# Layer 1's weights decoded on a fixed plan of steps: the scale product half a piece behind its maximum, the staging reloaded when the sign is taken

## The chip, the cores and the metric

One Trainium2 chip, one core. The metric is device time in microseconds (us): the median of several executions of the whole kernel. TensorE (PE; PEld is its weight load) multiplies, VectorE (DVE) and ScalarE (ACT) work elementwise, GpSimd (POOL) too but more slowly, and SyncE (SP) issues the transfers; each works off its own queue in order.

## What is computed

Attention with queries pooled by two, then two dense layers in a row. All inputs come as float64 and are kept to nearly float32 accuracy.

```python
# q, k, v: (4, 8, 1152, 64)
q_pool = q.reshape(B, H, S // 2, 2, D).mean(axis=3)
attn = softmax(q_pool @ k.T / sqrt(D))
x = (attn @ v).transpose(0, 2, 1, 3).reshape(2304, 512)
h = x @ w_in;   x = (h * cos(h)) @ w_out       # layer 1: 512 -> 2048 -> 512
h = x @ w_in2;  out = (h * sigmoid(h)) @ w_out2  # layer 2
```

## The kernel before, in words

Attention runs over 16 pairs of heads (four batches, four pairs each), each pair in nine tiles of 128 pooled queries, 144 tiles in all. A tile's scores are products of float16 halves (L545, L553), VectorE takes them out of PSUM with their minimum (L564), ACT makes the exponential (L572) and its high half (L578), POOL the low half (L583), SP transposes both (L585, `hl` to `hlT`), and four tiles later (`LAG`) TensorE multiplies them with v (L596, L600); after three tiles `group_end` divides and stores (L608 to L619).

Before a pair can start, `pair_prep` must have taken the maxima of its q, k and v (L120 to L482, tile `pm`), sent them through a product with a constant matrix (`scale_steps`, L104, tile `bm`) to get one scale for all partitions (L107 to L115), split q, k and v into halves (L460 to L509) and transposed them (L511, L521). This is spread over the tiles of the pair before.

The weights of layer 1 are 16 pieces of 1024 KB in float64: pieces 0 to 7 are of w_in, 8 to 15 of w_out. Each is loaded into one of three staging buffers (`wst`, L186) and decoded by `weight_steps`: ACT takes the absolute value of the upper word (L216, into `wt`) and low bits (L221); VectorE takes the maximum (L217), shifts the low bits in (L227) and the sign (L230); `mw` is the maximum as a number (L92), and its product `bm` gives the scale (L104 to L115); ACT writes the high half (L250) and the scaled value (L251), POOL the low half (L252). A `wt` buffer is held from L216 to L252; there are two of them.

Background work is a list of generators. `advance()` takes one step of each; it is called four times a tile, so a step is a quarter of a tile. The order in which instructions go into each engine's queue is made by a scheduler from their places in the program as priorities and from when they are ready. Products that share the PSUM tag "h" (two buffers) are the scale products of weights and pairs, and later layer 1's first products.

Before, a weight piece takes four steps: `decode(i + 1)` (three) and then `write(i)` (one), so the generator is through after 64 steps, 16 tiles. Layer 1 itself begins when the first block of attention's output is complete, in the 37th tile; `block_done` then calls `finish(wg)`.

Of the kernel before, what the change touches and what calls it, by code (L numbers as in the profile page):

```python
# [26 lines left out]
PSH = 15.0  # L27
NB_N, NB_SC, NB_H, NB_T, NB_S = 2, 4, 4, 4, 5
X_LAG = 40
W1_SUB, W1_BUFS, W1_AHEAD, WT_BUFS = 1, 3, 1, 2  # L30
W2_BUFS, W2_PACE = 3, 6
W2_TABLE = (("i", 0, 11, (0, 2, 5, 7, 10)), ("o", 88, 6, (0, 1, 3, 4, 6, 8, 9)))
PREP_POOL, GH_ACT, GH_TAIL = 0, 0, 0
# [3 lines left out]
R_AT = 1  # L37
NB_HK, NB_TT, NB_G, SIN_N = 2, 2, 2, 2
RATE = (0, 2, 2, 2)
LG, W_PACE, HI_N, HI_A = 12, 1, 2, 2  # L40
LAG = 4
GT = 3
TAIL_G = 4
# [4 lines left out]
def attention_moe_moe_kernel(ctx, tc, q, k, v, w_in1, w_out1, w_in2, w_out2, out):  # L48
# [3 lines left out]
    nc = tc.nc  # L52
# [30 lines left out]
    def scale_steps(m, pool, res, top, wide=False, apart=False, clean=False):  # L83

        n = m.shape[1]
        if wide:
            w = small.tile([128, 1], F32, name="mw", tag="mw")  # L90
            wi, mi = w.bitcast(I32), m.bitcast(I32)
            nc.vector.tensor_scalar(  # L92
                out=wi, in0=mi, scalar1=3, scalar2=EXP_MASK if clean else 0x3F800000, op0=ALU.logical_shift_left,
                op1=ALU.bitwise_and
            )
            if not clean:
                nc.vector.scalar_tensor_tensor(
                    out=wi, in0=mi, scalar=1 << 30, in1=wi, op0=ALU.bitwise_and, op1=ALU.bitwise_or
                )
            m = w  # L100
            if apart:
                yield
        bc = pool.tile([128, 2, GW], F32, tag="h", name="bm")[:, 0, 0:4]
        nc.tensor.matmul(bc[:, 0:n], mean, m, start=True, stop=True)  # L104
        yield
        s, u = res
        nc.vector.tensor_scalar(  # L107
            out=u, in0=bc[:, 0:n], scalar1=TINY, scalar2=2.0**(9 - top), op0=ALU.max, op1=ALU.mult
        )

        nc.vector.tensor_scalar(
            out=s.bitcast(I32), in0=u.bitcast(I32), scalar1=EXP_MASK, scalar2=EXP_MASK,
            op0=ALU.bitwise_and, op1=ALU.bitwise_xor,
        )
        nc.vector.tensor_scalar(  # L115
            out=u.bitcast(I32), in0=u.bitcast(I32), scalar1=EXP_MASK, scalar2=None, op0=ALU.bitwise_and
        )

    def absmax(out_, in_, axis=AX.X):
        nc.vector.tensor_reduce(out=out_, in_=in_, axis=axis, op=ALU.max, apply_absolute_value=True)  # L120
# [9 lines left out]
    def early(g, n):  # L130
        while True:
            with ahead(n):
                r = next(g, END)
            if r is END:
                return
            yield r
# [24 lines left out]
        w.ug = const.tile([128, 1], F32, name="ug" + tag)  # L161
        return w

    def weight_steps(w, srcs, stage, pspool, eng, nsub, bufs, ahead, wt_bufs=WT_BUFS):

        npc = w.npc  # L170
        wide = srcs[0].dtype != F32
        z = 2 if wide else 1
        srcs = [x.bitcast(I32) if wide else x for x in srcs]
        todo = [("i", p, h) for p in range(npc) for h in range(nsub)]
        todo += [("o", p, h) for p in range(npc) for h in range(nsub)]
        staged = []

        def shape(kind):
            return (NC // nsub, DFF // npc) if kind == "i" else (NF // nsub, DM // npc)

        def more():
            if todo:
                kind, p, h = todo.pop(0)
                c, n = shape(kind)
                st = stage.tile([128, c, n, z], I32 if wide else F32, tag="wst", name="wst", bufs=bufs)
                eng.dma_start(  # L186
                    out=st.rearrange("p c f z -> p c (f z)"),
                    in_=srcs[kind == "o"][c * 128 * h:c * 128 * (h + 1), p * n * z:(p + 1) * n * z].rearrange(
                        "(c p) f -> p c f", p=128
                    ),  # L190
                )
                staged.append(st)

        for _ in range(bufs):
            more()
        yield
        pieces = [(kind, p) for kind in "io" for p in range(npc)]
        decoded = []

        def decode(kind, p):  # L200
            c, n = shape(kind)
            s, u = (w.si, w.ui) if kind == "i" else (w.so, w.uo)
            s, u = s[:, p:p + 1], u[:, p:p + 1]
            m = small.tile([128, nsub], F32, name="wm", tag="wm", bufs=3)
            sts = [staged.pop(0) for _ in range(nsub)]
            ts = []
            for h, st in enumerate(sts):
                if not wide:
                    ts.append(st[:, :, :, 0])
                    absmax(m[:, h:h + 1], ts[-1], AX.XY)  # L210
                    yield
                    continue
                t = stage.tile([128, c, n], F32, tag="wt", name="wt", bufs=wt_bufs)
                ti = t.bitcast(I32)
                hf, low = st.bitcast(F32)[:, :, :, 1], st[:, :, :, 0]
                nc.scalar.activation(out=t, in_=hf, func=AF.Abs, scale=2.0**16)  # L216
                nc.vector.tensor_scalar(  # L217
                    out=t, in0=t, scalar1=W_MIN * 2.0**16, scalar2=None, op0=ALU.max, op1=ALU.max,
                    accum_out=m[:, h:h + 1]
                )  # L220
                nc.scalar.activation(  # L221
                    out=low, in_=st.rearrange("p c f z -> p c (f z)").bitcast(U16).rearrange(
                        "p c (f z) -> p c f z", z=4
                    )[:, :, :, 1], func=AF.Identity, scale=2.0**-13, bias=floor3
                )
                yield
                nc.vector.scalar_tensor_tensor(  # L227
                    out=ti, in0=ti, scalar=3, in1=low, op0=ALU.logical_shift_left, op1=ALU.bitwise_or
                )
                nc.vector.scalar_tensor_tensor(  # L230
                    out=ti, in0=st[:, :, :, 1], scalar=-(1 << 31), in1=ti, op0=ALU.bitwise_and, op1=ALU.bitwise_or
                )
                ts.append(t)
                yield
            m1 = m
            if nsub > 1:
                m1 = small.tile([128, 1], F32, name="wm1", tag="wm1", bufs=3)
                nc.vector.tensor_reduce(out=m1, in_=m, axis=AX.X, op=ALU.max)
            for _ in early(scale_steps(m1, pspool(), (s, u), 14, wide, clean=wide), P_CH):
                pass  # L240
            decoded.append(ts)
            yield

        def write(kind, p):
            c, n = shape(kind)
            hw, lw = (w.ih, w.il) if kind == "i" else (w.oh, w.ol)
            s = (w.si if kind == "i" else w.so)[:, p:p + 1]
            for h, t in enumerate(decoded.pop(0)):
                hi, lo = (x[:, c * h:c * (h + 1), p * n:(p + 1) * n] for x in (hw, lw))
                nc.scalar.activation(out=hi, in_=t, func=AF.Copy, scale=s)  # L250
                nc.scalar.activation(out=t, in_=t, func=AF.Copy, scale=s)  # L251
                nc.gpsimd.tensor_tensor(out=lo, in0=t, in1=hi, op=ALU.subtract)  # L252
                more()
                yield
            if (kind, p) == ("i", npc - 1):
                w.half = True

                nc.vector.tensor_reduce(out=w.kg, in_=w.si, axis=AX.X, op=ALU.min)
                nc.vector.tensor_reduce(out=w.ug, in_=w.ui, axis=AX.X, op=ALU.max)
                nc.vector.tensor_scalar(out=w.kg, in0=w.kg, scalar1=2.0**-15, scalar2=None, op0=ALU.mult)  # L260
                nc.vector.tensor_scalar(out=w.ug, in0=w.ug, scalar1=2.0**12, scalar2=None, op0=ALU.mult)

        for i in range(ahead):
            yield from decode(*pieces[i])
        for i, x in enumerate(pieces):
            if i + ahead < len(pieces):
                yield from decode(*pieces[i + ahead])
            yield from write(*x)

        r = npc // NC  # L270
        for e in range(r):
            pp = slice(e * (128 // r), (e + 1) * (128 // r))
            nc.vector.tensor_copy(w.uoT[pp, :], w.uo.rearrange("p (c e) -> p c e", e=r)[pp, :, e])
# [603 lines left out]
    if True:  # L877
# [76 lines left out]
        for n in range(2):  # L954
            P[n] = pair_new(at, *pairs[n])
            run_all(pair_loads(P[n]))
            if n == 0:
                wg = weight_steps(W1, (w_in1, w_out1), wst, lambda: ps_h, nc.sync, W1_SUB, W1_BUFS, W1_AHEAD)
                next(wg)
                run_all(pair_prep(at, P[0]))  # L960

# [2 lines left out]
                for _ in range(n):  # L964
                    yield

        wg = early(slowly(wg, W_PACE), P_W)
        bg.append(wg)

        def prep_then_load(n):  # L970
# [295 lines left out]
```

## Time and profile before

| | |
|---|---|
| median of 3 runs | 1396.19 us (1389.43 to 1397.52) |
| the profiled execution | 1396.53 us, its span 1394.7 us |
| PE busy | 1143.4 us (82%) |
| DVE busy | 1041.5 us (75%) |
| ACT busy | 871.6 us (62%) |
| POOL busy | 610.9 us (44%) |

The busy shares are means over stages that differ: in the first 280 us there is attention of the first batch and the weights of layer 1, then attention and layer 1 together, and from about 840 us on the dense layers.

### The profile page before, as it was taken

Reading aid. Unit: us, or ns where it says so; the run is one execution under the profiler, and the core shown is the slowest. Engines: PE = TensorE matmul, PEld = TensorE weight load, DVE = VectorE, ACT = ScalarE, POOL = GpSimd, SP = SyncE. Lnnn points to the kernel's source line nnn. Section 1 sums busy time; section 2 is a strip of 40 time slices with the busy share of each in tenths; the row PEclk is TensorE's granted clock in tenths of the full one; section 3 lists DMA queues with packets and bytes.
Section 4 is the critical chain, followed back from the end, with each engine's and each line's share of the span. In section 5 each row is a group of like instructions: output and inputs, shape, how many; then the busy total and the mean of one; then the engine's idle time right before and its main releaser. Section 6 shows DMA issues by size and latency. Waiting matters only on the chain. (4 is left out here: it accounts for less than half of the span.)

```text
span 1394.7 us, 26446 instructions
## 1 busy us (share of the span) xinstructions
PE 1143.4 (82%) x10668; PEld 915.2 (66%) x10668; DVE 1041.5 (75%) x1927; ACT 871.6 (62%) x1061; POOL 610.9 (44%) x352
## 2 busy tenths in 40 slices
PE   2464355588898778898898989999898999999998
PEld 1243133366676456666666767888787888888887
DVE  6976897769788689877999897796756764444483
ACT  5867686668686678768678876453636643343352
POOL 2457365527556655665665645433567400000000
PEclk9566568889999978999999999999999999999999
DMA  9899759986989999989699986332336000000001
GB/s 287 176 224 211 204 102 196 201 163 118 187 151 185 200 204 176 201 171 175 135 198 210 200 159 137 91 92 76 76 76 152 31 24 15 25 17 16 17 31 31
DMA packets 509593, 186.26 MB, mean 134 GB/s; under 512 B 465952, under 2 KB 484384, under 8 KB 509472
## 3 DMA queue, kind: packets, MB, share of 16 engines
q1 hardware_dynamic: 509472, 184.59, 64.2%
q8 instruction: 83, 1.36, 0.4%
q14 instruction: 38, 0.31, 0.1%
HBM read 66.58 MB, written 9.44 MB: 55 GB/s over the span
## 5 line engine op out<-in xcount | busy, mean ns | idle before, releaser
L583 POOL TENSOR_TENSOR hl<-sc,hl 128x1152 f16<-128x1152 f32 x144 | 363.6, 2534 | 212.5 <-ACT hl L578 119.1
L545 PE MATMUL sp<-kT,qT 128*128 128x512 f16 (+1 forms) x768 | 196.6, 375 | 98.1 <-DVE sc L564 83.0
L564 DVE TENSOR_SCALAR_CACHE_REDUCE sc<-sp,psu 128x512 f32<-128x512 f32 (+1 forms) x288 | 229.1, 808 | 39.5 <-PE sp L545 34.3
L596 PE MATMUL pv<-vt,hlT 128*128 128x130 f16 (+1 forms) x1440 | 196.7, 238 | 73.5 <-DMA hlT<-hl 66.4
L681 PEld LDWEIGHTS <-ih 128*128 128x128 f16 x2304 | 226.0, 99 | 40.7 <-issue 10.6
L572 ACT ACTIVATE sc<-sc,nb 128x1152 f32<-128x1152 f32 x144 | 179.7, 1249 | 95.2 <-DVE nb L569 81.5
L596 PEld LDWEIGHTS <-hlT 128*128 128x128 f16 (+1 forms) x1440 | 146.6, 110 | 105.1 <-DMA hlT<-hl 82.4
L681 PE MATMUL h<-ys,ih 128*128 128x256 f16 x1152 | 194.7, 273 | 5.1 <-ACT gs L697 5.1
L681 PE MATMUL h<-xT,ih 128*128 128x256 f16 x1024 | 188.8, 278 | 0.2 <-DMA xT<-xn 0.2
L600 PE MATMUL pv<-vt,hlT 128*128 128x65 f16 (+1 forms) x1440 | 188.7, 208 | 0.0
L545 PEld LDWEIGHTS <-qT 128*128 128x128 f16 x768 | 77.1, 109 | 167.2 <-issue 133.8
L578 ACT ACTIVATE hl<-sc 128x1152 f16<-128x1152 f32 x144 | 165.1, 1155 | 11.5 <-DMA hlT<-hl 5.4
L736 PE MATMUL y<-gh,oh 128*128 128x256 f16 x576 | 160.2, 278 | 7.1 <-ACT y L745 7.1
L736 PE MATMUL y<-gl,oh 128*128 128x256 f16 x576 | 160.1, 278 | 2.5 <-POOL gl L725 2.5
L736 PE MATMUL y<-gh,ol 128*128 128x256 f16 x576 | 160.4, 278 | 0.0
L850 PEld LDWEIGHTS <-op 128*128 128x128 f16 x1512 | 147.7, 98 | 18.1 <-issue 0.6
L681 PE MATMUL h<-ys,il 128*128 128x256 f16 x576 | 157.2, 273 | 0.0
L600 PEld LDWEIGHTS <-hlT 128*128 128x128 f16 (+1 forms) x1440 | 142.9, 108 | 17.0 <-issue 7.9
L681 PE MATMUL h<-xT,il 128*128 128x256 f16 x512 | 142.0, 277 | 0.0
L736 PEld LDWEIGHTS <-oh 128*128 128x128 f16 x1152 | 113.7, 100 | 26.2 <-issue 9.2
L725 POOL TENSOR_TENSOR gl<-tt,gh 128x1024 f16<-128x1024 f32 x36 | 92.4, 2566 | 78.2 <-DVE gh L724 71.9
L681 PEld LDWEIGHTS <-il 128*128 128x128 f16 x1152 | 113.7, 99 | 16.6 <-issue 1.3
(310 smaller groups left out, 2028.7 us busy)
## 6 DMA issues: line engine op xcount, KB each, us to landing
wst<-in_moe_w_in_dram SPq DMA_DIRECT2D x16, 1024.0 KB, 6.6
stk<-in_k_dram SPq DMA_DIRECT2D x32, 288.0 KB, 3.8
stv<-in_v_dram SPq DMA_DIRECT2D x32, 288.0 KB, 4.3
stq<-in_q_dram SPq DMA_DIRECT2D x32, 256.0 KB, 3.1
wst<-in_moe_w_out_dram SPq DMA_DIRECT2D x8, 1024.0 KB, 6.1
wst<-in_moe_w_out_dram SPq DMA_DIRECT2D x16, 512.0 KB, 6.2
ydr<-y SPq DMA_DIRECT2D x9, 512.0 KB, 3.7
y32b<-ydr SPq DMA_DIRECT2D x9, 512.0 KB, 3.3
```

Of the source, the lines that this page charges most:

```text
L545: nc.tensor.matmul(sp[:, o - a:o - a + n], P.qT[e][:, t, :], kT[:, o:o + n], start=(e == 0), stop=(e == 1))
L564: nc.vector.tensor_scalar(out=T.sc[:, a:z], in0=sp, scalar1=T.P.su, scalar2=None, op0=ALU.mult, op1=ALU.min, accum_out=mx[:, x:x + 1],)
L572: nc.scalar.activation(out=T.sc, in_=T.sc, func=AF.Exp, scale=-1.0, bias=nb)
L578: nc.scalar.activation(out=hi, in_=T.sc, func=AF.Copy)
L583: nc.gpsimd.tensor_tensor(out=T.hl[:, 1, :], in0=T.sc, in1=T.hl[:, 0, :], op=ALU.subtract)
L596: nc.tensor.matmul(G.pv[r, T.gi], T.hlT[:, 0, c, r], P.vt[i][:, c], start=(c == 0), stop=(c == KC - 1), skip_group_check=True,)
L600: nc.tensor.matmul(G.pv[r, T.gi, 0], T.hlT[:, 1, c, r], P.vt[i][:, c, 0], start=False, stop=(c == KC - 1), skip_group_check=True,)
L681: nc.tensor.matmul(hp, wt[:, c, f * 128:(f + 1) * 128], xt(c), start=(i == 0), stop=(i == 3 * NC - 1), skip_group_check=True,)
L725: nc.gpsimd.tensor_tensor(out=G.gl, in0=t, in1=gh, op=ALU.subtract)
L736: nc.tensor.matmul(blk.y[:, oc, :], wt[:, f, oc * 128:(oc + 1) * 128], gt[:, f % 4, :], start=(f == 0 and e == 0 and oc % 2 == 0), stop=(f ...
L850: nc.tensor.matmul(bank, t[:, e, c, :], wt[:, c, :], start=start, stop=True, skip_group_check=True)
```

## The change

`weight_steps` is replaced by `layer1_weight_steps`, which works from a table `W1_TABLE = (6, (0, 2, 4, 8, 11))`: piece p starts at step 6p, and its five parts stand 0, 2, 4, 8 and 11 steps later. The parts are: absolute value, low bits and maximum (0); the shift (2); the sign, the load of the next piece into the staging buffer just read, and `mw` (4); the scale product and the three operations behind it (8); the writes (11). Sorted by step, the last part of piece 15 is step 101. Before, the load was issued behind a piece's writes, and the scale product directly behind `mw`. There are three `wt` buffers instead of two. The instructions of a piece, their shapes and their engines are the same.

```diff
-W1_SUB, W1_BUFS, W1_AHEAD, WT_BUFS = 1, 3, 1, 2
+W1_BUFS, WT_BUFS = 3, 3
+W1_TABLE = (6, (0, 2, 4, 8, 11))
...
+    def layer1_weight_steps(w, srcs, stage, pspool, eng, bufs, wt_bufs, period, offs):
...
+        def piece_steps(kind, p):
...
+            nc.scalar.activation(out=t, in_=hf, func=AF.Abs, scale=2.0**16)
+            nc.scalar.activation(out=low, in_=high16, func=AF.Identity, scale=2.0**-13, bias=floor3)
+            nc.vector.tensor_scalar(
+                out=t, in0=t, scalar1=W_MIN * 2.0**16, scalar2=None, op0=ALU.max, op1=ALU.max, accum_out=m
+            )
+            yield
+            nc.vector.scalar_tensor_tensor(
+                out=ti, in0=ti, scalar=3, in1=low, op0=ALU.logical_shift_left, op1=ALU.bitwise_or
+            )
+            yield
+            nc.vector.scalar_tensor_tensor(
+                out=ti, in0=st[:, :, :, 1], scalar=-(1 << 31), in1=ti, op0=ALU.bitwise_and, op1=ALU.bitwise_or
+            )
             more()
...
+            sc = scale_steps(m, pspool(), (s, u), 14, True, True, True)
+            next(sc)
+            yield
+            next(sc)
+            run_all(sc)
+            yield
+            hi, lo = (x[:, :, p * n:(p + 1) * n] for x in ((w.ih, w.il) if kind == "i" else (w.oh, w.ol)))
+            nc.scalar.activation(out=hi, in_=t, func=AF.Copy, scale=s)
+            nc.scalar.activation(out=t, in_=t, func=AF.Copy, scale=s)
+            nc.gpsimd.tensor_tensor(out=lo, in0=t, in1=hi, op=ALU.subtract)
...
+        events = []
         for i, x in enumerate(pieces):
-            if i + ahead < len(pieces):
-                yield from decode(*pieces[i + ahead])
-            yield from write(*x)
-
+            g = []
+            events += [(i * period + o, len(events) + k, x, g) for k, o in enumerate(offs)]
+        events.sort(key=lambda x: x[:2])
+        now = 0
+        for when, _, x, g in events:
+            while now < when:
+                now += 1
+                yield
+            if not g:
+                g.append(piece_steps(*x))
+            next(g[0])
...
-        wg = early(slowly(wg, W_PACE), P_W)
+        wg = early(wg, P_W)
```

## Rows read from the trace of the kernel before

**Rows 1.** The page's slices of the span, TensorE: busy tenths in 40 equal slices.
```profile
PE   2464355588898778898898989999898999999998
```
**Rows 2.** Windows: stretch, length, busy time of each engine, clock, DMA share, GB/s.
```profile
0.00:280.00 280.00, 132.62 (x1064) 83.29 (x1064) 220.77 (x479) 191.74 (x212) 145.61 (x90) 0.71 0.92 200
280.00:560.00 280.00, 236.24 (x2306) 178.15 (x2307) 228.88 (x465) 210.82 (x251) 153.85 (x84) 0.92 0.93 173
```
**Rows 3.** Timeline of ACT, exponentials of tiles 18, 19, 27, 28, 37.
```profile
123.07 1.24 ACT L572 ACTIVATE sc<-sc,nb 128x1152 f32<-128x1152 f32 x1
...
174.33 1.24 ACT L572 ACTIVATE sc<-sc,nb 128x1152 f32<-128x1152 f32 x1
...
209.53 1.24 ACT L572 ACTIVATE sc<-sc,nb 128x1152 f32<-128x1152 f32 x1
...
221.89 1.25 ACT L572 ACTIVATE sc<-sc,nb 128x1152 f32<-128x1152 f32 x1 [3.00 <-DVE nb L569]
...
261.38 1.25 ACT L572 ACTIVATE sc<-sc,nb 128x1152 f32<-128x1152 f32 x1 [5.90 <-DVE nb L569]
```
**Rows 4.** Timeline of TensorE, 149 to 168 us: scale products and scores.
```profile
149.57 0.59 PE L104 MATMUL bm<-mw,mean 128*128 128x1 f32 x2 [3.55 <-DVE mw L92]
150.01 0.57 PE L104 MATMUL bm<-pm,mean 128*128 128x3 f32 x2
163.98 0.58 PE L104 MATMUL bm<-mw,mean 128*128 128x1 f32 x2 [13.39 <-DVE mw L92]
164.53 2.93 PE L545 MATMUL sp<-kT,qT 128*128 128x512 f16 x8
```
**Rows 5.** Timeline of VectorE: two stretched instructions, a pair's maxima, a sign, a scale.
```profile
37.54 3.24 DVE L227 SCALAR_TENSOR_TENSOR wt<-wt,wst 128x1024 int32<-128x1024 int32 x1
...
81.85 0.14 DVE L482 TENSOR_REDUCE pm<-pm 128x2 f32<-128x4 f32 x1
...
84.53 0.14 DVE L481 COPY pm<-pm 128x1 f32<-128x1 f32 x1
...
105.19 1.21 DVE L230 SCALAR_TENSOR_TENSOR wt<-wst,wt 128x1024 int32<-128x1024 int32 x1
...
150.63 0.15 DVE L107 TENSOR_SCALAR uo<-bm 128x1 f32<-128x1 f32 x1
...
196.21 3.04 DVE L230 SCALAR_TENSOR_TENSOR wt<-wst,wt 128x1024 int32<-128x1024 int32 x1
```
**Rows 6.** Windows: four stretches of the first stage, columns as in rows 2.
```profile
20.00:88.00 68.00, 34.81 (x214) 20.51 (x215) 60.12 (x124) 46.49 (x48) 33.99 (x17) 0.67 0.93 212
88.00:124.00 36.00, 22.18 (x214) 14.90 (x213) 27.88 (x73) 33.84 (x39) 27.40 (x15) 0.77 1.03 216
124.00:174.00 50.00, 16.63 (x104) 11.42 (x105) 39.02 (x74) 31.99 (x37) 19.10 (x11) 0.51 0.88 210
174.00:222.00 48.00, 24.96 (x206) 15.04 (x205) 42.87 (x84) 33.81 (x39) 30.34 (x14) 0.66 0.64 118
```
**Rows 7.** Windows: sum of 20 to 40 and 40 to 60 us.
```profile
sum 40.00, PE 21.46 PEld 11.85 DVE 39.50 ACT 30.18 POOL 16.09; mean PE 10.73 PEld 5.93 DVE 19.75 ACT 15.09 POOL 8.05
```
**Rows 8.** Lines' instructions: count, ns min/median/max, first and last start us.
```profile
L227 DVE SCALAR_TENSOR_TENSOR wt<-wt,wst x16: 1209/1592/3242, 20.4 to 193.6; 128x1024 int32<-128x1024 int32 x16
...
L230 DVE SCALAR_TENSOR_TENSOR wt<-wst,wt x16: 1187/1219/3039, 23.4 to 196.2; 128x1024 int32<-128x1024 int32 x16
...
L252 POOL TENSOR_TENSOR ol<-wt,oh x8: 2119/2381/3106, 134.4 to 212.3; 128x1024 f16<-128x1024 f32 x8
```
**Rows 9.** Windows of L227, then of L230 alone: sums over 20 to 262 us.
```profile
sum 242.00, DVE 31.01; mean DVE 6.20
...
sum 242.00, DVE 24.93; mean DVE 4.99
```
**Rows 10.** Timeline of SP: the load of piece 9.
```profile
106.51 0.37 SPq L186 DMA_DIRECT2D wst<-in_moe_w_out_dram  x1
```
**Rows 11.** Waits of the DMA queue on SP, 0 to 280 us: sum, times, longest.
```profile
SPq L186 <- DVE wt L230: 18.9, 7, 8.3
```

More of the change, by code (lines that the diff above doesn't have):

```diff
@@ L39 @@
 RATE = (0, 2, 2, 2)
-LG, W_PACE, HI_N, HI_A = 12, 1, 2, 2
+LG, HI_N, HI_A = 12, 2, 2
 LAG = 4
@@ L162, in new_w @@
         return w
-    def weight_steps(w, srcs, stage, pspool, eng, nsub, bufs, ahead, wt_bufs=WT_BUFS):
+    def layer1_weight_steps(w, srcs, stage, pspool, eng, bufs, wt_bufs, period, offs):
         npc = w.npc
[L171 to L175, printed above, removed]
+        srcs = [x.bitcast(I32) for x in srcs]
+        pieces = [(kind, p) for kind in "io" for p in range(npc)]
+        todo = list(pieces)
@@ L176, in weight_steps @@
         staged = []
-        def shape(kind):
-            return (NC // nsub, DFF // npc) if kind == "i" else (NF // nsub, DM // npc)
         def more():
[L182 to L192, printed above, removed]
@@ L194, in weight_steps @@
-        for _ in range(bufs):
-            more()
[L196 to L202, printed above, removed]
-            s, u = s[:, p:p + 1], u[:, p:p + 1]
[L204 to L241, printed above, removed]
-            yield
@@ L244, in write @@
[L244 to L254, printed above, removed]
+            if not todo:
+                return
@@ new lines, in more @@
+            kind, p = todo.pop(0)
+            c, n = (NC, DFF // npc) if kind == "i" else (NF, DM // npc)
+            st = stage.tile([128, c, n, 2], I32, tag="wst", name="wst", bufs=bufs)
+            eng.dma_start(
+                out=st.rearrange("p c f z -> p c (f z)"),
+                in_=srcs[kind == "o"][:, p * n * 2:(p + 1) * n * 2].rearrange("(c p) f -> p c f", p=128),
+            )
+            staged.append(st)
+        def piece_steps(kind, p):
+            st = staged.pop(0)
+            c, n = st.shape[1], st.shape[2]
+            m = small.tile([128, 1], F32, name="wm", tag="wm", bufs=3)
+            t = stage.tile([128, c, n], F32, tag="wt", name="wt", bufs=wt_bufs)
+            ti = t.bitcast(I32)
+            hf, low = st.bitcast(F32)[:, :, :, 1], st[:, :, :, 0]
+            high16 = st.rearrange("p c f z -> p c (f z)").bitcast(U16).rearrange("p c (f z) -> p c f z", z=4)[:, :, :, 1]
+            nc.scalar.activation(out=t, in_=hf, func=AF.Abs, scale=2.0**16)
[10 more added lines that the diff above has]
+                out=ti, in0=st[:, :, :, 1], scalar=-(1 << 31), in1=ti, op0=ALU.bitwise_and, op1=ALU.bitwise_or
+            )
+            more()
+            s, u = ((w.si, w.ui) if kind == "i" else (w.so, w.uo))
+            s, u = s[:, p:p + 1], u[:, p:p + 1]
+            sc = scale_steps(m, pspool(), (s, u), 14, True, True, True)
+            next(sc)
+            yield
+            next(sc)
[5 more added lines that the diff above has]
+            nc.gpsimd.tensor_tensor(out=lo, in0=t, in1=hi, op=ALU.subtract)
@@ L261, in write @@
                 nc.vector.tensor_scalar(out=w.ug, in0=w.ug, scalar1=2.0**12, scalar2=None, op0=ALU.mult)
-        for i in range(ahead):
-            yield from decode(*pieces[i])
-        for i, x in enumerate(pieces):
-            if i + ahead < len(pieces):
-                yield from decode(*pieces[i + ahead])
-            yield from write(*x)
+            yield
+        for _ in range(bufs):
+            more()
+        yield
+        events = []
+        for i, x in enumerate(pieces):
+            g = []
[5 more added lines that the diff above has]
+                now += 1
+                yield
+            if not g:
+                g.append(piece_steps(*x))
+            next(g[0])
         r = npc // NC
@@ L957, in attention_moe_moe_kernel @@
             if n == 0:
-                wg = weight_steps(W1, (w_in1, w_out1), wst, lambda: ps_h, nc.sync, W1_SUB, W1_BUFS, W1_AHEAD)
+                wg = layer1_weight_steps(W1, (w_in1, w_out1), wst, lambda: ps_h, nc.sync, W1_BUFS, WT_BUFS, *W1_TABLE)
                 next(wg)
```

## The prediction

> **What bounds the kernel now.** I read the page's slices first: TensorE is at 2 to 6 tenths in the first eight of 40 slices and at 8 or 9 later [rows 1]. The windows say the same: 132.6 us of TensorE work in the first 280 us, 236.2 in the next 280 [rows 2]. So the end of the kernel is set by work that starts late; what the first stage loses is lost at the end too, and what it gains should come through one to one, because all behind it (layer 1, layer 2) hangs on attention's tiles and has no clock of its own.
>
> Then I asked how the first stage's tiles follow each other, by the exponentials of ACT (one a tile) [rows 3]. Tile 18 starts its exponential at 123.1 us and tile 19 at 174.3; tile 27 at 209.5 and tile 28 at 221.9. Those are the hand-overs from head pair 1 to 2, **51.3 us**, and from 2 to 3, 12.4 us. Within a pair nine tiles take 35.2 us (174.3 to 209.5, eight steps of 4.4). So one hand-over holds some 39 us in which attention stands still.
>
> Why it does: TensorE's timeline [rows 4]. Pair 2's first scores start at 164.5. Its own scale product (bm<-pm) ran at 150.0, right behind a weight piece's product (bm<-mw) at 149.6. But the maxima that it needs were in place at 84.7 (L482 at 81.9, L481 at 84.5 [rows 5]): 65 us early. What held it is the order of the products. They all use the tag "h" with two buffers, and the trace has them in program order to the piece. A step is one call of advance(), four to a tile. Before, piece p's product stands at step 4p+2 (step 3 for piece 0); pair 2's stands at step 36+11 = 47, so pieces 0 to 11 come first, and piece 11 is the fourth of w_out: VectorE takes its scale (uo) at 150.6, just behind that product [rows 5]. The plan before asks for twelve pieces within the first 47 steps, and the engines had done eight when pair 1 ran out of tiles (w_out's first POOL write, piece 8, starts at 134.4 [rows 8]).
>
> VectorE is the engine nearest its limit there: over 20 to 222 us it is busy 60.1 + 27.9 + 39.0 + 42.9 = 169.9 of 202 us, a share of 0.84; by stretch 0.88, 0.77, 0.78 and 0.89 [rows 6]. ACT is busy 46.5 + 33.8 + 32.0 + 33.8 = 146.1 us, 0.72, and at 0.94 only in 88 to 124 [rows 6].
>
> **The change, part by part.** *The plan.* Piece p begins at step 6p, its product stands at 6p+8, its last step at 6p+11: 101 for piece 15, the 26th tile, instead of about 64. Pair 2's product (step 47) now comes behind pieces 0 to 6 only, pair 1's (step 11) behind piece 0 where it stood behind pieces 0 to 2, pair 3's (step 83) behind pieces 0 to 12. Seven pieces is less than the eight that were done when pair 1 ended, so the 51.3 us should shrink to a hand-over like the other, 12.4: 39 us of standing still go.
>
> They are not all gained, because decoding worked in them: 39.0 us of VectorE [rows 6] move beside attention. The sum is therefore made by VectorE's work, which does not change: 169.9 us have to be done between 20 us and the point that now lies at 222. What is gained is idle time, 202 - 169.9 = 32.1 us at most.
>
> *The share that VectorE can reach.* No stretch shows the new mix for long. The bound below is 0.88, the stretch in which attention and decoding ran side by side with one hand-over [rows 6]; the bound above is 39.5 of 40 us, 0.98, in 20 to 60 us, where decoding and tiles filled each other's gaps [rows 7]. I take 0.92, nearer to the lower row, since two of the four stretches read 0.88 and 0.89 and hand-overs remain.
>
> *The two-input instructions.* L227 and L230 took 1.2 us at the least and up to 3.2 and 3.0 [rows 8]; all 32 sum to 31.0 + 24.9 = 55.9 us [rows 9] where 32 x 1.21 would be 38.7: 17.2 us of stretching. It lies in 12 of the 32, which took over 1.5 us, the first at 37.5 and the last at 196.2 [rows 5]: 1.43 us each. They are stretched when POOL works. POOL was busy 0.38 of the stretch 124 to 174 and 0.60 of the other three together (34.0 + 27.4 + 30.3 of 152) [rows 6]; the 12 instructions that ran in the first would move to the second: 12 x 0.22 x 1.43 = 4 us more. Bounds: nothing, and all 20 others stretched, 28.6.
> The Trainium skill (SBUF — State Buffer, "Who interferes with whom") states that a VectorE instruction with two SBUF inputs contends with a GpSimd instruction that reads SBUF, and that the one that issues second waits for the whole of the other. The rows fit it, and it speaks against the change, which lays such instructions under POOL's subtractions; taken at its hardest it is the third rival.
>
> *The sum.* (169.9 + 4) / 0.92 = 189.0 us instead of 202: 13.0 gained. By the share alone: 0.88 gives 197.6, 4 gained; 0.98 gives 177.4, 25 gained.
>
> *The product half a piece behind its maximum.* The same two matmuls and four small operations; mw is made a tile earlier, so the product no longer waits on TensorE for it. TensorE stood 13.4 us before the product at 164.0 [rows 4], but that lies in the standing time counted above. What waits is ACT's write of the piece, 7 steps behind its sign. Nothing of attention needs it. Taken at 0; cover: the third wt buffer, whose slot is wanted again at step 6p+18, seven steps (1.75 tiles, some 12 us at 189 us for 27 tiles, by the sum above) after the last step. Without that cover the next piece would wait, not attention.
>
> *The reload at the sign.* I expect nothing of it. The load at 106.51 went out as soon as the sign taken at 105.19 (1.21 us long) was done [rows 5, 10]: the scheduler had already put it there, ahead of its place in the program. It keeps SP's queue waiting as before: 18.9 us in seven waits, the longest 8.3 [rows 11]. Queued behind are the transposes of hl (L585), qT and kT, and behind those TensorE's L596. If all 13 reloads waited 2.7 us, 16 us more on SP; if none, 19 less. Taken at 0, since the tile's second product is issued four tiles (16 us and more) after its scores, longer than the longest wait.
>
> *The writes' end.* Weights are complete in tile 26 where the last write now starts at 212.3 us, behind tile 27 [rows 3, 8]. Layer 1 asks for them when the first block is done, tile 37 (261.4 [rows 3]): ten tiles, over 40 us, of cover.
>
> The profiled execution took 1396.5 us around a span of 1394.7; the median of three is 1396.2. **Forecast: 1396.5 - 13.0 = 1383.5 us.**
>
> **The rivals.** *More.* VectorE at 0.98 and no added stretching: 169.9 / 0.98 = 173.4, 28.6 gained, 1368 us. For it: pair 1's product frees itself two pieces earlier too, and ACT has room (146.1 us at its best share of 0.94 would be 155). Against: both in-order engines would have to be lucky at once.
>
> *Nothing.* The standing time is spread instead of removed: VectorE stays at 0.86, 173.9 / 0.86 = 202, 1396.5 us. For it: the 0.77 of 88 to 124, with hardly any standing tile [rows 6], and that half of the change (the reload) is in the trace already. Against: the gap has one cause, seen to the piece, and the plan takes it away.
>
> *Slower: the stretching decides.* All 20 unstretched two-input instructions come under POOL: (169.9 + 28.6) / 0.92 = 215.8, 13.8 lost, 1410 us. It decides from 15.9 us on, 11 of the 20. For it: half of L227 are stretched now. Against: POOL would have to be busy nearly all the time; it was at 0.60.
>
> **How the numbers follow.** Forecast 0.45, more 0.20, nothing 0.25, slower 0.10. One per cent, 14 us, is about what a measurement of this kernel can tell from no change; three runs before spread over 8. Below 1382 lie the second case and somewhat under half of the first: 0.42. Above 1410 lies most of the third rival and a little of disorder in the later order of work: 0.10. Within: 0.48. The range leaves out the far half of the case of more and the slower one's end: 1367 to 1402.
>
> **What would show it.** Right: the step from tile 18's exponential to tile 19's at 10 to 15 us; bm<-pm of pair 2 before 110 us and behind the seventh bm<-mw; VectorE at 0.9 or more from 20 us to tile 28, which starts near 209; the reload still right behind the sign. Wrong, if tile 28 comes as late as now with no single gap (nothing), if L227 and L230 sum to well over 60 us (stretching), or if tile 28 is early and the end isn't: then a later stage has its own limit and the first premise falls.

## The result, and the profile after

| | before | after |
|---|---|---|
| median | 1394.97 us (4 runs) | 1377.1 us (4 runs, 1374.58 to 1377.37) |
| ratio | | 0.9873, 95% interval 0.984 to 0.9906 |
| profiled execution | 1396.53 us, span 1394.7 | 1377.37 us, span 1375.3 |

Faster by 1.3%, and the interval stays clear of 1. The forecast was 13.0 us less than the profiled execution; it is 19.2 less (17.9 by the medians).

The page's slices, TensorE: the first stage is still the thin one [rows 1], but the eighth slice is at 8 where it was at 5.

```profile
PE   1554656888998778888898889998999999999998
```

The changed kernel's timeline of ACT, exponentials of tiles 18, 19, 27, 28 and 37:

```profile
141.71 1.24 ACT L548 ACTIVATE sc<-sc,nb 128x1152 f32<-128x1152 f32 x1
148.10 1.25 ACT L548 ACTIVATE sc<-sc,nb 128x1152 f32<-128x1152 f32 x1 [3.08 <-DVE nb L545]
...
192.91 1.26 ACT L548 ACTIVATE sc<-sc,nb 128x1152 f32<-128x1152 f32 x1 [0.36 <-DVE nb L545]
199.99 1.26 ACT L548 ACTIVATE sc<-sc,nb 128x1152 f32<-128x1152 f32 x1 [1.38 <-DVE nb L545]
...
238.23 1.26 ACT L548 ACTIVATE sc<-sc,nb 128x1152 f32<-128x1152 f32 x1 [0.38 <-DVE nb L545]
```

Against [rows 3]: the hand-over of 51.3 us is 6.4, the next 7.1 instead of 12.4. Tile 18 comes 18.6 us *later* than before. Eleven pieces' products run ahead of it where it was eight, so pair 1 now shares the engines with more decoding; that this is the cause was not tested. Tile 19 comes 26.2 us earlier, tile 28 21.9 and tile 37 23.1.

Its timeline of VectorE, the last of pair 2's maxima, then of TensorE, the scale products of pairs 2 and 3:

```profile
74.32 0.15 DVE L457 COPY pm<-pm 128x1 f32<-128x1 f32 x1
```

```profile
92.77 0.33 PE L105 MATMUL bm<-mw,mean 128*128 128x1 f32 x2
...
93.50 0.36 PE L105 MATMUL bm<-pm,mean 128*128 128x3 f32 x2
...
162.68 0.38 PE L105 MATMUL bm<-mw,mean 128*128 128x1 f32 x2
162.92 0.36 PE L105 MATMUL bm<-pm,mean 128*128 128x3 f32 x2
```

Pair 2's product runs at 93.5 instead of 150.0 [rows 4]. The order is as counted: it is right behind the seventh product of a piece, pair 3's behind the thirteenth. The gate is narrower, not gone: pair 2's maxima are in place at 74.5, so its product still stands 19 us behind pieces, where it was 65. Pair 1's tiles run until 141.7 and cover that.

Windows of the changed kernel, the stretches of [rows 6] (PE, PEld, VectorE, ACT, POOL):

```profile
20.00:88.00 68.00, 30.77 (x154) 16.20 (x154) 58.56 (x121) 46.18 (x48) 34.28 (x14) 0.75 0.84 200
88.00:124.00 36.00, 20.82 (x192) 14.43 (x192) 36.00 (x74) 32.43 (x37) 24.19 (x13) 0.69 1.13 220
124.00:174.00 50.00, 29.83 (x252) 18.78 (x253) 44.44 (x102) 41.11 (x46) 37.20 (x19) 0.70 1.11 249
174.00:222.00 48.00, 30.17 (x246) 19.53 (x246) 44.14 (x101) 38.60 (x47) 29.75 (x17) 0.68 0.96 187
```

VectorE has no idle time at all in 88 to 124 us and is at 0.89 in 124 to 174, where it was at 0.78; TensorE's 16.6 us there are 29.8.

Two pairs of windows hold the sum, first of the kernel before, then of the changed one: up to tile 28 and from there to tile 37 (before, the second half and the sum of both).

```profile
221.90:261.40 39.50, 21.98 (x220) 14.38 (x219) 26.27 (x68) 26.44 (x31) 22.65 (x12) 0.83 1.09 205
sum 241.40, PE 120.46 PEld 76.15 DVE 196.15 ACT 172.47 POOL 133.49; mean PE 60.23 PEld 38.07 DVE 98.08 ACT 86.23 POOL 66.74
```

```profile
20.00:200.00 180.00, 97.53 (x709) 59.60 (x710) 161.46 (x345) 140.52 (x153) 110.20 (x54) 0.70 1.00 218
200.00:238.20 38.20, 23.92 (x225) 15.04 (x224) 32.54 (x74) 29.70 (x36) 29.38 (x15) 0.81 0.97 182
```

To tile 37, VectorE does 196.2 us of work in 241.4 before and 161.5 + 32.5 = 194.0 in 218.2 after: shares of 0.81 and 0.89. The work is nearly the same, the idle time falls from 45.2 to 24.2.

### The profile page after: what moved, and what is told of

It is laid out like the page before. It is cut to its first block, busy times and chain, and to the rows that moved or that the text cites. A ratio compares the mean times of both kernels' runs of the same rounds, so it can differ in the third digit from the quotient of the medians.

```text
span 1375.3 us, 26440 instructions
## 1 busy us (share of the span) xinstructions
PE 1152.2 (84%) x10668; PEld 917.7 (67%) x10668; DVE 1046.8 (76%) x1927; ACT 871.6 (63%) x1061; POOL 624.3 (45%) x352
## 5 line engine op out<-in xcount | busy, mean ns | idle before, releaser
L559 POOL TENSOR_TENSOR hl<-sc,hl 128x1152 f16<-128x1152 f32 x144 | 370.1, 2581 | 170.1 <-ACT hl L554 94.2
L572 PEld LDWEIGHTS <-hlT 128*128 128x128 f16 (+1 forms) x1440 | 148.0, 111 | 92.3 <-DMA hlT<-hl 64.4
L554 ACT ACTIVATE hl<-sc 128x1152 f16<-128x1152 f32 x144 | 164.7, 1154 | 26.7 <-DMA hlT<-hl 13.3
L712 PE MATMUL y<-gl,oh 128*128 128x256 f16 x576 | 163.0, 283 | 0.4 <-POOL gl L701 0.4
L576 PEld LDWEIGHTS <-hlT 128*128 128x128 f16 (+1 forms) x1440 | 144.7, 109 | 19.3 <-issue 11.4
```

The lines of the kernel that those rows point to most:

```text
L554: nc.scalar.activation(out=hi, in_=T.sc, func=AF.Copy)
L559: nc.gpsimd.tensor_tensor(out=T.hl[:, 1, :], in0=T.sc, in1=T.hl[:, 0, :], op=ALU.subtract)
L572: nc.tensor.matmul(G.pv[r, T.gi], T.hlT[:, 0, c, r], P.vt[i][:, c], start=(c == 0), stop=(c == KC - 1), skip_group_check=True,)
L576: nc.tensor.matmul(G.pv[r, T.gi, 0], T.hlT[:, 1, c, r], P.vt[i][:, c, 0], start=False, stop=(c == KC - 1), skip_group_check=True,)
L712: nc.tensor.matmul(blk.y[:, oc, :], wt[:, f, oc * 128:(oc + 1) * 128], gt[:, f % 4, :], start=(f == 0 and e == 0 and oc % 2 == 0), stop=(f ...
```

## The experiments

Every run was timed beside the kernel before on the same chip, so the ratios are what compares. The changed kernel stands at 0.9873.

| kernel | median us | ratio to before, 95% |
|---|---|---|
| before, own bank for the pieces' products | 1374.35 | 0.9893 (0.9851 to 0.9935) |
| before, six steps a piece | 1387.28 | 0.9958 (0.9936 to 0.998) |
| before, three `wt` buffers | 1384.67 | 0.996 (0.9942 to 0.9978) |
| before, reload at the sign | 1394.94 | 1.0018 (0.9995 to 1.0042) |
| before, six steps and three `wt` | 1376.6 | 0.9873 (0.9833 to 0.9913) |
| after, two `wt` buffers | 1393.04 | 0.9994 (0.9971 to 1.0017) |
| after, product right behind `mw` | 1380.42 | 0.9898 (0.9858 to 0.9938) |
| after, own bank | 1372.35 | 0.9852 (0.9798 to 0.9906) |
| after, maximum twice | 1385.45 | 0.9953 (0.9928 to 0.9978) |
| after, absolute value twice | 1398.32 | 1.0044 (1.0013 to 1.0074) |
| after, four steps a piece | 1376.65 | 0.9883 (0.9836 to 0.993) |
| before, own bank and three `wt` | 1376.35 | 0.9882 (0.9827 to 0.9936) |

**Is it the order of the products?** Layer 1's accumulator in PSUM is unused while weights are decoded; the pieces' products go there and no longer take turns with the pairs'.

```diff
+        class OwnBank:
+            def tile(self, shape, dtype, tag, name):
+                return ps_y.tile([128, NC, GW], F32, tag="y", name=name)
-                wg = weight_steps(W1, (w_in1, w_out1), wst, lambda: ps_h, nc.sync, W1_SUB, W1_BUFS, W1_AHEAD)
+                wg = weight_steps(W1, (w_in1, w_out1), wst, lambda: OwnBank(), nc.sync, W1_SUB, W1_BUFS, W1_AHEAD)
```

> The kernel before, with the scale products of the weight pieces in a PSUM buffer of their own (layer 1's accumulator, unused until then) instead of the two buffers of tag h that the pairs' scale products share. Theory (the order of the products holds pair 2): pair 2's product no longer stands behind pieces 0 to 11 and runs before 110 us, the step from tile 18's exponential to tile 19's falls from 51.3 us to under 20, and the time falls by at least half of what the change gave, to 1387 us or less, though the plan, the third wt buffer and the place of the reload are as before. Rival (the pieces' own pace is the limit: wt buffers, staging, or VectorE's work): the gap moves or stays, and the time is within 5 us of 1395.

The timeline of TensorE in this kernel, pair 2's product, and that of ACT, tiles 18 and 19:

```profile
85.75 0.54 PE L104 MATMUL bm<-pm,mean 128*128 128x3 f32 x2
86.14 0.57 PE L104 MATMUL bm<-mw,mean 128*128 128x1 f32 x2
```

```profile
124.51 1.26 ACT L572 ACTIVATE sc<-sc,nb 128x1152 f32<-128x1152 f32 x1 [1.75 <-DVE pm L481]
...
127.76 1.24 ACT L572 ACTIVATE sc<-sc,nb 128x1152 f32<-128x1152 f32 x1
```

VectorE's timeline has the last of pair 2's maxima here:

```profile
82.40 0.15 DVE L481 COPY pm<-pm 128x1 f32<-128x1 f32 x1
```

Pair 2's product runs 3.2 us after its maxima are in place, where it was 65. The hand-over is 3.3 us, and no difference in time to the changed kernel is shown, with none of the change in this one. The theory's three numbers held. The gate is shown.

**Is it the pace of the plan, or the third buffer?** Two runs, one part each.

```diff
                 nc.gpsimd.tensor_tensor(out=lo, in0=t, in1=hi, op=ALU.subtract)
                 more()
-                yield
+                for _ in range(3):
+                    yield
```

> The kernel before with two empty steps more behind each piece's writes, so that a piece takes six steps as in the changed kernel; two wt buffers, product right behind mw, load behind the writes. Pair 2's product then stands behind pieces 0 to 7 instead of 0 to 11. Theory (the plan's pace is what counts): most of the gain, 1376 to 1384 us, and tile 18 to tile 19 under 20 us. Rival (the third wt buffer or the product half a piece later carries the gain): 1390 us or more.

```diff
-W1_SUB, W1_BUFS, W1_AHEAD, WT_BUFS = 1, 3, 1, 2
+W1_SUB, W1_BUFS, W1_AHEAD, WT_BUFS = 1, 3, 1, 3
```

> The kernel before with three wt buffers instead of two, nothing else. Theory: pieces get ahead a little in the first 18 tiles, but twelve of them still stand before pair 2's product; the gap shrinks by some 10 us at most, the time is 1388 to 1397 us. Rival (the buffers held the pieces back, and that was the gap): 1375 to 1382 us.

Six steps, timeline of ACT, tiles 18, 19, 27, 28:

```profile
128.95 1.24 ACT L573 ACTIVATE sc<-sc,nb 128x1152 f32<-128x1152 f32 x1
141.49 1.25 ACT L573 ACTIVATE sc<-sc,nb 128x1152 f32<-128x1152 f32 x1 [1.03 <-DVE nb L570]
...
178.09 1.24 ACT L573 ACTIVATE sc<-sc,nb 128x1152 f32<-128x1152 f32 x1
219.80 1.25 ACT L573 ACTIVATE sc<-sc,nb 128x1152 f32<-128x1152 f32 x1 [5.65 <-DVE nb L570]
```

Three buffers, tiles 18 and 19:

```profile
128.28 1.26 ACT L572 ACTIVATE sc<-sc,nb 128x1152 f32<-128x1152 f32 x1 [0.46 <-DVE so L111]
...
164.75 1.24 ACT L572 ACTIVATE sc<-sc,nb 128x1152 f32<-128x1152 f32 x1
```

Each gives about a third of the gain. The slower pace opens pair 2's gate (12.5 us) and moves the standing time to pair 3's (41.7 us), where fourteen pieces must be through. The third buffer alone leaves 36.5 us at pair 2's. My expectation of "most of the gain" for the pace was wrong. For the buffers it held only in part: the gap shrank by 14.8 us, not 10 at most, and the median of 1384.7 lies below the 1388 to 1397 given, though the ratio of 0.996 would make it 1389 beside the 1395 of the result's table.

**Both, and the change without its buffer.** First the two edits above together:

> The kernel before with six steps a piece and three wt buffers, the load still behind the writes and the product still right behind mw. With two buffers six steps alone gave 1387 us: the step from tile 18 to 19 fell to 12.5 us, but tile 27 to 28 rose to 41.7, because pair 3's product stands behind 14 pieces that were not done. Theory (the pace opens the first gate, the third buffer lets the pieces keep that pace and opens the second): both hand-overs under 15 us and 1374 to 1381 us, as the changed kernel. Rival (the product half a piece behind its maximum is what lets the pieces keep up): tile 27 to 28 stays over 25 us and the time at 1383 us or more.

```diff
-W1_BUFS, WT_BUFS = 3, 3
+W1_BUFS, WT_BUFS = 3, 2
```

> The changed kernel with two wt buffers instead of three. Theory: the pieces fall behind their plan, pair 3's product (behind 13 pieces) comes late, tile 27 to 28 over 20 us, 1382 to 1390 us. Rival (the plan's offsets do without the third buffer, since a piece's last step 6p+11 lies before 6p+12): within 4 us of the changed kernel's 1377.

Six steps with three buffers, ACT, tiles 18, 19, 27, 28:

```profile
143.34 1.24 ACT L573 ACTIVATE sc<-sc,nb 128x1152 f32<-128x1152 f32 x1
146.09 1.24 ACT L573 ACTIVATE sc<-sc,nb 128x1152 f32<-128x1152 f32 x1
...
191.90 1.26 ACT L573 ACTIVATE sc<-sc,nb 128x1152 f32<-128x1152 f32 x1 [1.97 <-DVE nb L570]
199.12 1.26 ACT L573 ACTIVATE sc<-sc,nb 128x1152 f32<-128x1152 f32 x1 [3.88 <-DVE so L111]
```

The change with two buffers: TensorE, the last piece's product ahead of pair 3's, and ACT, tiles 27 and 28:

```profile
184.38 0.59 PE L105 MATMUL bm<-mw,mean 128*128 128x1 f32 x2 [3.81 <-DVE mw L93]
184.82 0.57 PE L105 MATMUL bm<-pm,mean 128*128 128x3 f32 x2
```

```profile
166.83 1.26 ACT L548 ACTIVATE sc<-sc,nb 128x1152 f32<-128x1152 f32 x1 [0.39 <-DVE so L112]
...
209.23 1.24 ACT L548 ACTIVATE sc<-sc,nb 128x1152 f32<-128x1152 f32 x1
```

Pace and buffer together, with the reload and the product where they were, give the ratio of the change, 0.9873. So these two are enough, and two buffers had been what kept the six steps from their pace. The change without its third buffer shows no gain, less than my theory's 1382 to 1390 us: pair 3 stands for 42.4 us behind a product that ran at 184.4 (162.7 in the changed kernel).

**The two parts that are named in the change.** The reload moved alone:

```diff
+                more()
                 ts.append(t)
                 yield
...
                 nc.gpsimd.tensor_tensor(out=lo, in0=t, in1=hi, op=ALU.subtract)
-                more()
```

> The kernel before with the staging buffer's reload issued behind the sign instead of behind the writes, nothing else. Theory: no change, within 4 us of 1395, since the reload already goes out when the sign is taken. Rival (the early reload carries part of the gain): 5 us faster or more, and ACT's waits for loads fall.

No change. Every engine's queue, SP's too, holds the same instructions in the same order with this edit as without it: the scheduler had given the load that place already. The product at offset 4, right behind `mw`:

```diff
-W1_TABLE = (6, (0, 2, 4, 8, 11))
+W1_TABLE = (6, (0, 2, 4, 4, 11))
```

> The changed kernel with the scale product at offset 4, right behind mw, instead of 8. Theory: the product's place on TensorE costs nothing by itself, within 5 us of 1377; it would also stand behind no more pieces for pair 2 (pieces 0 to 7 instead of 0 to 6). Rival (TensorE, in order, waits for the maximum and holds up scores): 1383 us or more, with more wait of bm for mw than the 25 us of the changed kernel.

Pair 2's product stands behind eight pieces here, one more than in the changed kernel, not "no more". The hand-overs are 2.7 and 7.2 us, TensorE's wait of `bm` for `mw` is 24.4 us (25.0 in the changed kernel). The intervals overlap: no difference is shown.

**What sets the pace of the stage now?** An instruction of each piece made twice, with the same values left behind: the maximum on VectorE, then the absolute value on ACT.

```diff
+            nc.vector.tensor_scalar(
+                out=t, in0=t, scalar1=W_MIN * 2.0**16, scalar2=None, op0=ALU.max, op1=ALU.max, accum_out=m
+            )
```

> The changed kernel with the maximum of each piece taken twice (the second time over what the first left, so nothing else changes): 16 x 1.29 = 20.6 us more on VectorE in the first stage. Theory (the stage is worked off at the pace of VectorE, busy 0.89 of 20 to 238 us): the end moves by 15 to 23 us, to 1392 to 1400 us. Rival (the stage is held by the order of products and the hand-overs between engines, and VectorE has slack where it counts): 8 us or less, 1385 us at most.

```diff
             nc.scalar.activation(out=t, in_=hf, func=AF.Abs, scale=2.0**16)
+            nc.scalar.activation(out=t, in_=hf, func=AF.Abs, scale=2.0**16)
```

> The changed kernel with the absolute value of each piece taken twice by ACT: 16 x 1.12 = 17.9 us more on ACT in the first stage. Theory (VectorE sets the pace, ACT is busy 0.78 of 20 to 238 us): 6 us or less, 1383 us at most. Rival (ACT is as much the bound): 12 us or more, 1389 us.

Windows from 20 us to tile 37, the maximum twice and the absolute value twice:

```profile
20.00:252.10 232.10, 120.53 (x919) 76.78 (x920) 207.34 (x455) 171.20 (x188) 132.37 (x68) 0.70 0.94 204
```

```profile
20.00:260.20 240.20, 124.49 (x927) 77.73 (x927) 186.33 (x424) 186.71 (x204) 133.44 (x68) 0.69 0.90 197
```

The maximum: VectorE's work rises by 13.3 us (207.3 against 194.0; other instructions are stretched less), tile 37 comes 13.9 us later, at the same share of 0.89. That fits VectorE setting the pace, but does not show it alone: the maximum lies in the chain of each piece too, and the hand-over to pair 3 rises from 7.1 to 13.2 us. At the end 11 us are left (0.0080 of 1392), between what the two theories gave. The absolute value: 16.5 us more of ACT, and tile 37 comes 22.0 us later, with VectorE at 0.78; at the end it is 24 us (0.0171 of 1392). My theory that ACT had room falls with it. Where it goes is the same gate, ACT's timeline, tiles 27 and 28:

```profile
183.72 1.24 ACT L549 ACTIVATE sc<-sc,nb 128x1152 f32<-128x1152 f32 x1
...
213.59 1.25 ACT L549 ACTIVATE sc<-sc,nb 128x1152 f32<-128x1152 f32 x1 [4.46 <-DVE nb L546]
```

The absolute value is the head of a piece's chain (ACT, VectorE, TensorE, VectorE, ACT). Made longer, it puts the thirteenth product at 189.9 and pair 3 behind it: 29.9 us for a hand-over. Tile 27 is 9.2 us earlier than in the changed kernel, so the whole loss lies in that hand-over. I read it so that the pieces' chain, through the gate, paces the stage here, and that a share of 0.78 on ACT was no slack; the run that would part the chain from ACT's work, the same edit with the pieces' products in a buffer of their own, was not made.

**Is the pace needed with the rest of the change? And the gate gone with three buffers?**

```diff
-W1_TABLE = (6, (0, 2, 4, 8, 11))
+W1_TABLE = (4, (0, 1, 2, 5, 7))
```

> The changed kernel with four steps a piece as before (offsets 0, 1, 2, 5, 7), three wt buffers and the reload at the sign kept. Pair 2's product stands behind pieces 0 to 10 again. Theory (pace and buffers both count): the step from tile 18 to 19 is back over 25 us, 1382 to 1390 us, near the 1384.7 of the kernel before with three wt buffers. Rival (the early offsets and the buffers are enough, the pace is not needed): within 4 us of 1377.

Timeline of ACT, tiles 18 and 19:

```profile
128.64 1.24 ACT L548 ACTIVATE sc<-sc,nb 128x1152 f32<-128x1152 f32 x1
...
160.45 1.25 ACT L548 ACTIVATE sc<-sc,nb 128x1152 f32<-128x1152 f32 x1
```

The gap is back as expected (31.8 us) and tile 37 starts at 247.0, 8.8 us later than in the changed kernel; yet the end is the same: the time that I expected (1382 to 1390 us) is missed, and the rival's is met. From tile 37 to tile 144 this execution takes 587.3 us, the changed kernel's 595.6, that of the kernel before 592.7. So the trace shows that the pace closes the gap, and the time does not show that it is needed: with three buffers and the early offsets, four steps a piece end as early. Why this ends 8 us before the kernel before with three `wt` buffers was not followed.

The own bank and the three `wt` buffers on the kernel before, both edits as above:

> The kernel before, four steps a piece, with three wt buffers and the pieces' products in a PSUM buffer of their own. Theory: with the gate gone neither plan nor pace is needed; no hand-over over 13 us; weights done by 215 us instead of 254 with two buffers, so the early gain of the own buffer at tile 37 (32 us) is kept: 1365 to 1372 us. Rival (the stage's work is the limit and it is used up already): 1372 to 1378 us, like the changed kernel with or without the own buffer.

1376 us, no hand-over over 6.5 us, tile 37 at 241.4, 20.0 us earlier than before and not 32: the rival's number. The own bank on the changed kernel, the same edit:

> The changed kernel with the pieces' scale products in the PSUM buffer of their own. Theory: with the plan no pair's product waits long for a piece, so little is left to gain: 1370 to 1380 us, and no hand-over over 13 us. Rival (the shared tag still costs the changed kernel as much as it cost before): under 1365 us.

1372 us and hand-overs of 6.5 and 4.5 us, as the theory had it, and tile 37 at 243.4. It has the lowest ratio of all, but its interval holds that of the changed kernel; no version is shown to beat it.

## Why the prediction was right, and where its steps were off

*The gate.* Right, and shown from both sides: the own bank takes it away without the plan, two `wt` buffers bring it back with the plan, at pair 3. The number of products ahead of pair 2's fell from twelve to seven as counted, and the hand-over to 6.4 us, less than the 10 to 15 given.

*The sum.* The mis-sized term is the idle time that could be won: "202 - 169.9 = 32.1 us at most", counted to tile 28 with all the work done by then and everything behind it as before. The share up to tile 28 came to 161.5 / 180 = 0.90, under the 0.92 taken; but 161.5 us of work were done there instead of 173.9, so that tile 28 came at 200.0 and not near 209. The end of the decoding (the last piece's shift and sign and the copies of the scales of w_out, 5.4 us) ran between tiles 28 and 37, where VectorE went from 26.3 of 39.5 us (0.67) to 32.5 of 38.2 (0.85). Counted to tile 37 the idle time is 45.2 us, and (196.2 + 4) / 0.92 would have given 23.8 gained; 23.1 were. That this comes so near is luck: the work was 194.0 us and not 200.2, the share 0.89 and not 0.92, and the two misses cancel.

*Through to the end one to one.* Roughly. 23.1 us at tile 37 are 20.2 at tile 144 (833.85 against 854.08) and 19.2 at the end. Over the kernels of this study the stretch from tile 37 to tile 144 takes 585 to 601 us without any edit in it; a gain of the first stage is known at the end to within some 8 us. Not all of it is the order of the work: the kernel with its reload moved has the same order on every engine as the kernel before, and its execution took 587.2 us there against 592.7. What else differs in that stretch was not followed.

*The two-input instructions.* The third rival stayed small. Windows of L202 and of L206 alone, sums over 20 to 262 us:

```profile
sum 242.00, DVE 29.42; mean DVE 29.42
...
sum 242.00, DVE 28.86; mean DVE 28.86
```

58.3 us against 55.9 [rows 9]: 2.3 more where 4 were taken (2.8 with the part of the first L202 that lies before 20 us). The Trainium skill's rule (SBUF — State Buffer, "Who interferes with whom") is borne out in the longest single cases, 3.39 and 3.33 us against 1.21 alone: both start just behind a subtraction of POOL and last about as long as the rest of it and 1.21 us. It comes up a little oftener, in 15 of the 32 over 1.5 us where it was 12. The term itself was read a little off: 11 of the 32 started between 124 and 174 us, not 12, and three of these were stretched already.

*The reload: nothing.* Right as to the time. As a sign it was too strong: the load goes out within 0.3 us of the end of the sign in 8 of 13 cases before and in 6 after, and up to 11.4 us later in the others. *The product half a piece behind: nothing.* No difference was measured.

*The third buffer, in the prediction only the cover of the product's later place: "Without that cover the next piece would wait, not attention."* Wrong, and the step that the prediction got most clearly wrong. It is true that the next piece waits, but pair 3's product stands behind thirteen pieces, so attention waits with it: without the buffer pair 3's hand-over is 42.4 us and no gain is left (0.9994). I had the chain written down for pair 2 and did not follow it for the piece that waits for its buffer.

*The reload's queue.* SP waited for the sign 16.2 us in five waits, against 18.9 in seven [rows 11]:

```profile
SPq L180 <- DVE wt L206: 16.2, 5, 9.5
```

## What to carry to other kernels

When two streams of work share a small rotating buffer, their order of allocation is a gate: look for an instruction that runs long after its inputs were ready, right behind one of the other stream, and count which of them. Spreading the other stream out opens the gate only if that stream can keep its own pace; test the pace and the buffers that allow it apart and together, since each alone may only move the wait to the next gate. And read a first stage's gain at a mark in the work where it ends (a tile), beside the end of the kernel, where later work and the single execution add several microseconds of their own. The mark has to lie behind all of the stage's work: with the own bank on the kernel before, tile 37 came 31.9 us early while VectorE decoded until 252.7, and the execution's span was 24.7 us shorter.

## What was not expected of the hardware

VectorE's share over the stage came out the same, 0.89, with 194.0 and with 207.3 us of work, so time followed its work in these two; with the absolute value twice it was 0.78. ACT at a share of 0.78 looked idle enough for 17.9 us more, and that cost 22.0 us at tile 37. The likely cause, argued from the place of the loss and not tested by itself, is that the added instruction lies at the head of a chain that three buffers allow only so far ahead.
